# Finer phase steps merged by fractional position, and a reworked attention tail, in a four-layer attention/GLU kernel

## The chip, the cores and the metric

The kernel runs on one core of one Trainium2 chip. The time is the device time in microseconds of that core, one whole execution. The kernel before took 2078.02 us in the median of the twelve executions that ran beside the changed kernel (2074.32 to 2080.72).

Engines: TensorE (PE in the profile; PEld is its weight load), VectorE (DVE), ScalarE (ACT), GpSimd (POOL), SyncE (SP, which here only issues transfers).

## The reference, cut to what matters

```python
def _A_ref(x, wqkv, wo):              # attention, H = 32 heads of Dh = 32
    ...
    W, dil = 8, 2                     # each token sees 8 keys: itself, 2 back, 4 back, ... 14 back
    kg = k[:, :, idx_c, :]; vg = v[:, :, idx_c, :]
    logits = jnp.einsum("bhsd,bhswd->bhsw", q, kg) * scale     # masked where idx < 0
    attn = softmax(logits)
    o = jnp.einsum("bhsw,bhswd->bhsd", attn, vg)
    return o.reshape(B, S, D) @ wo

def _B_ref(x, W_gate, W_up, W_down):  # gated unit, F = 3584
    h = relu(x @ W_gate) * (x @ W_up)
    return h @ W_down

x = A_x                               # 1 x 2048 x 1024, bf16
x = x + _A_ref(layernorm(x), ...);  x = x + _B_ref(layernorm(x), ...)
x = x + _A_ref(layernorm(x), ...);  x = x + _B_ref(layernorm(x), ...)
```

## The kernel before

Each of the four layers works through four blocks of 512 tokens. An *item* is one layer and one block. Layers 0 and 2 are attention, 1 and 3 are the gated unit (GLU). An attention item has a phase (projections q, k, v; logits L; softmax) and a tail (expand, multiply by v, add, output projection). The tail is *deferred*: its steps are interleaved with the phase steps of the next item. So the tail of a layer's last attention item runs inside the first GLU block of the next layer; I call that block *mixed* and the other three *plain*.

The logits. `prod` is q times eight shifted copies of k, and TensorE sums it over the 32 dimensions of a head with a constant matrix `wide`, in column groups of 32:

```python
        def prod_red(c):                       # c: one of 8 groups of 4 heads
            ...
                prod = a_pool.tile([P, W, BLK], BF16, ...)
                nc.vector.tensor_tensor(prod[:], q..., k shifted 8 ways..., op=ALU.mult)   # cut
                for tq in range(TPB):          # 4
                    for w in range(W):         # 8
                        nc.tensor.matmul(Lt[32 * tq:32 * tq + 32, w, :], lhsT=wide[...],
                                         rhs=prod[:, w, tq * P:(tq + 1) * P], ...,
                                         tile_position=(0, 32 * tq))        # 32 matmuls of 128 columns
```

The tail. TensorE repeats the attention weights over a head's 32 dimensions (`E`, in PSUM, two buffers of two banks). VectorE multiplies E by shifted v, straight out of PSUM. GpSimd makes the first add of a tree of three, VectorE the other two:

```python
        def pv(c):
            ...
                for tqp in range(2):
                    tt = tl_pool.tile([P, 2, W, P], BF16, tag="t", ..., bufs=3)
                    for wh in range(2):
                        e = psum_e.tile([P, 2, BLK], F32, tag="E", name="E")      # 2 banks, bufs=2
                        for j in range(2):
                            nc.tensor.matmul(e[:, j, :], lhsT=eexp[...], rhs=a[...], ...)
                        nc.vector.tensor_tensor(tt[:, :, 4*wh:4*wh+4, :], e[:]..., vsh, op=ALU.mult)
                    nc.gpsimd.tensor_tensor(tt[:, :, 0:4, :], tt[:, :, 0:4, :], tt[:, :, 4:8, :], op=ALU.add)
                    nc.vector.tensor_tensor(tt[:, :, 0:2, :], tt[:, :, 0:2, :], tt[:, :, 2:4, :], op=ALU.add)
                    nc.vector.tensor_tensor(oT[...], tt[:, :, 0, :], tt[:, :, 1, :], op=ALU.add)
```

The order. Every engine executes its own instructions in the order of the compiled program. That follows the order in which the kernel emits them, but not strictly: some instructions are pulled forward where an engine would wait. Steps are coarse (one step is three projections, or a whole `pv`), and the layer norm of the next item goes in as one lump:

```python
            merged = _interleave(ph, prev_tl)          # by count
            pos = (len(merged) * 3) // 5
            merged = merged[:pos] + nln + merged[pos:] # layer norm of the next item, as a lump
            run(merged)
```

The down projection of the GLU (`down(half)`) accumulates in two tiles of two banks, from the same pool as E. Weights go through a ring of five slabs (`wring`), loaded by SyncE.

## Time and profile before

I cut the profiled execution into stages. A stage of attention runs from the first E matmul of one tail to the first E matmul of the next tail. A GLU block ends with the last residual add of its down projection. The first columns of each layer, before its first E, are the *heads*.

| before, us | heads (2) | attention items (6) | mixed GLU blocks (2) | plain GLU blocks (6) | sum |
|---|---|---|---|---|---|
| whole stage | 164.2 | 620.2 | 380.0 | 907.4 | 2071.8 |
| one of it | 99.3 and 64.9 | 103.4 | 190.0 | 151.2 | |

The page of the kernel before, its first and fourth part (busy time of the engines; the chain of work that ended last, by engine):

```profile
span 2075.1 us, 24471 instructions
...
PE 1891.8 (91%) x10496; PEld 862.3 (42%) x10496; DVE 824.0 (40%) x1050; ACT 528.6 (25%) x809; POOL 388.1 (19%) x311
...
PE 60%; DVE 16%; POOL 14%; issue 5%; ACT 4%; POOLq 0%; DVEq 0%; ACTq 0%
```

TensorE looks full over the whole span, yet it is only 60% of the chain. The average hides two regimes, which the table by stretches separates. Kernel before, one attention item and one plain GLU block; columns after the comma are the busy time of PE, PEld, DVE, ACT and POOL (with instruction counts), then the granted TensorE clock, the share of the DMA engines and GB/s:

```profile
197.10:303.30 106.20, 87.08 (x608) 39.82 (x608) 77.86 (x91) 32.16 (x50) 50.16 (x34) 0.95 0.24 80
750.60:903.30 152.70, 149.21 (x706) 67.95 (x704) 25.31 (x42) 33.76 (x53) 1.11 (x2) 0.99 0.46 145
```

The GLU block is TensorE, 149 of 153 us. In the attention item no engine is full: TensorE idles 19 us, VectorE 28. The kernel before, what engines waited for (total us, times, longest):

```profile
POOL t L309 <- DVE t L307: 532.0, 127, 52.0
...
DVE t L310 <- POOL t L309: 161.4, 120, 2.4
...
PE E L303 <- DVE t L307: 92.4, 78, 2.8
...
PE tp L186 <- ACT xn L182: 42.1, 16, 22.8
...
PE L L250 <- DVE prod L245: 13.6, 11, 2.0
```

Read upwards, this is a ring. E waits for VectorE's multiply (L307) to free its PSUM buffer. VectorE's queue is in order, so a multiply stands behind the small adds (L310) of the tile before it, and those wait for the GpSimd add (L309), which waits for the multiplies. VectorE's 161.4 us of waiting are about 20 us a tail; with 77.9 us of work that is 98 of the 106 us of an item.

The kernel before, groups by shape (busy us, mean ns of one, idle time before them and what ended it):

```profile
L309 POOL TENSOR_TENSOR t<-t 128x1024 bf16<-128x1024 bf16 x128 | 332.8, 2600 | 534.0 <-DVE t L307 532.0 <-DVE oT L311 2.0
L307 DVE TENSOR_TENSOR t<-E,v 128x1024 bf16<-128x1024 f32 x256 | 305.5, 1216 | 0.4 <-PE E L303 0.4
...
L245 DVE TENSOR_TENSOR prod<-q,k 128x4096 bf16<-128x4096 bf16 x64 | 155.8, 2434 | 68.8 <-ACT k L225 68.3
```

The kernel before, timeline of an item (start, duration, engine, line):

```profile
209.29 2.12 POOL L309 TENSOR_TENSOR t<-t 128x1024 bf16<-128x1024 bf16 x1 [1.53 <-DVE t L307]
209.32 4.23 DVE L245 TENSOR_TENSOR prod<-q,k 128x4096 bf16<-128x4096 bf16 x1
...
215.15 2.34 DVE L307 TENSOR_TENSOR t<-E,v 128x1024 bf16<-128x1024 f32 x2
216.51 2.12 POOL L309 TENSOR_TENSOR t<-t 128x1024 bf16<-128x1024 bf16 x1 [2.90 <-DVE t L307]
...
220.33 2.29 DVE L245 TENSOR_TENSOR prod<-q,k 128x4096 bf16<-128x4096 bf16 x1
220.37 4.23 POOL L309 TENSOR_TENSOR t<-t 128x1024 bf16<-128x1024 bf16 x1 [1.60 <-DVE t L307]
```

`prod` takes 2.29 us and the GpSimd add 2.12. Started together, whichever is second takes 4.23, about the sum of both: they do not share, one stands still. The multiplies out of PSUM at 215.15 are not slowed beside the GpSimd add (two in 2.34). The Trainium skill ("SBUF — State Buffer", section "SBUF: two separate sides") says just this: the port pair common to VectorE and GpSimd is an exclusive lock held for a whole instruction, taken by VectorE operations with two SBUF inputs against a GpSimd operation that reads SBUF. This trace agrees, with the numbers above.

The start of the kernel before (ACTq is ScalarE's instruction stream issuing transfers):

```profile
0.80 8.15 ACTq L121 DMA_DIRECT2D x<-in_A_x_dram  x8
...
9.04 1.28 ACT L160 ACT_TABLE_LOAD   x1 [9.04 <-DMA x<-in_A_x_dram]
```

### The profile page before, as it was taken

Reading aid. Unit: us, or ns where it says so; the run is one execution under the profiler, and the core shown is the slowest. Engines: PE = TensorE matmul, PEld = TensorE weight load, DVE = VectorE, ACT = ScalarE, POOL = GpSimd, SP = SyncE. Lnnn points to the kernel's source line nnn. Section 1 sums busy time; section 2 is a strip of 40 time slices with the busy share of each in tenths; the row PEclk is TensorE's granted clock in tenths of the full one; section 3 lists DMA queues with packets and bytes.
Section 4 is the critical chain, followed back from the end, with each engine's and each line's share of the span. In section 5 each row is a group of like instructions: output and inputs, shape, how many; then the busy total and the mean of one; then the engine's idle time right before and its main releaser. Section 6 shows DMA issues by size and latency. Waiting matters only on the chain.

```text
span 2075.1 us, 24471 instructions
## 1 busy us (share of the span) xinstructions
PE 1891.8 (91%) x10496; PEld 862.3 (42%) x10496; DVE 824.0 (40%) x1050; ACT 528.6 (25%) x809; POOL 388.1 (19%) x311
## 2 busy tenths in 40 slices
PE   4978787888999999999998788878999999999999
PEld 2534343433444444444444333333344444444444
DVE  1576767765121111111126777777541111210220
ACT  7623241412223023023033232323122130120110
POOL 1063535333000000000011535363320000000000
PEclk9999999999999999999999898999999999999999
DMA  5313131332444444444442131313335544544542
GB/s 186 123 61 102 61 102 61 102 112 92 152 152 129 155 149 142 152 152 135 143 142 68 55 102 61 102 62 121 114 113 161 162 133 152 172 140 153 174 142 92
DMA packets 246269, 253.44 MB, mean 122 GB/s; under 512 B 4400, under 2 KB 241968, under 8 KB 246160
## 3 DMA queue, kind: packets, MB, share of 16 engines
q1 hardware_dynamic: 245008, 249.77, 37.7%
q8 instruction: 82, 1.34, 0.3%
q10 hardware_dynamic: 1152, 2.10, 0.3%
q14 instruction: 27, 0.22, 0.0%
HBM read 247.46 MB, written 4.19 MB: 121 GB/s over the span
## 4 chain that ended last, share of the span: by engine, by line
PE 60%; DVE 16%; POOL 14%; issue 5%; ACT 4%; POOLq 0%; DVEq 0%; ACTq 0%
PE dacc L389 18%; PE acc_u L359 17%; PE acc_g L359 16%; POOL t L309 14%; DVE t L307 9%; PE acc_wo L323 2%; DVE t L310 2%; DVE prod L245 2%; PE acc_v L216 1%; PE acc_k L216 1%; PE acc_q L216 1%; ACT junk L160 1%; PE L L250 1%; ACT xn L182 1%; ACT xnT L187 1%
## 5 line engine op out<-in xcount | busy, mean ns | idle before, releaser
L359 PE MATMUL acc_u<-xnT,wu 128*128 128x512 bf16 x1792 | 428.8, 381 | 11.3 <-DVE hT L365 10.9
L359 PE MATMUL acc_g<-xnT,wg 128*128 128x512 bf16 x1792 | 435.6, 386 | 0.8 <-ACT xnT L187 0.6
L309 POOL TENSOR_TENSOR t<-t 128x1024 bf16<-128x1024 bf16 x128 | 332.8, 2600 | 534.0 <-DVE t L307 532.0
L389 PE MATMUL dacc<-wd,hT 128*128 128x512 bf16 x1792 | 388.1, 379 | 0.0
L365 DVE TENSOR_TENSOR hT<-acc_u,r 128x512 bf16<-128x512 f32 x224 | 154.8, 691 | 561.9 <-PE acc_u L359 511.0
L364 ACT ACTIVATE r<-acc_g 128x512 bf16<-128x512 f32 x224 | 133.5, 596 | 774.2 <-PE acc_g L359 774.2
L307 DVE TENSOR_TENSOR t<-E,v 128x1024 bf16<-128x1024 f32 x256 | 305.5, 1216 | 0.4 <-PE E L303 0.4
L359 PEld LDWEIGHTS <-wu 128*128 128x128 bf16 x1792 | 175.1, 98 | 227.4 <-issue 24.0
L359 PEld LDWEIGHTS <-wg 128*128 128x128 bf16 x1792 | 175.6, 99 | 220.6 <-issue 21.5
L389 PEld LDWEIGHTS <-hT 128*128 128x128 bf16 x1792 | 175.3, 98 | 211.5
L303 PE MATMUL E<-a,eexp 32*128 32x512 bf16 x512 | 104.8, 398 | 95.7 <-DVE t L307 92.4
L245 DVE TENSOR_TENSOR prod<-q,k 128x4096 bf16<-128x4096 bf16 x64 | 155.8, 2434 | 68.8 <-ACT k L225 68.3
L393 DVE TENSOR_TENSOR x<-dacc,x 128x512 bf16<-128x512 f32 x64 | 41.2, 686 | 349.8 <-PE dacc L389 349.8
L216 PE MATMUL acc_k<-xnT,wk 128*128 128x512 bf16 x512 | 141.3, 403 | 0.8 <-DVE x L326 0.8
L216 PE MATMUL acc_q<-xnT,wq 128*128 128x512 bf16 x512 | 131.6, 390 | 1.7 <-ACT xnT L187 1.7
L216 PE MATMUL acc_v<-xnT,wv 128*128 128x512 bf16 x512 | 130.6, 394 | 0.2 <-ACT q L220 0.2
L323 PE MATMUL acc_wo<-wo,oT 128*128 128x512 bf16 x512 | 114.6, 379 | 9.3 <-DVE x L326 9.3
L160 ACT ACTIVATE junk<-x 128x1024 bf16<-128x1024 bf16 x64 | 67.5, 1055 | 202.3 <-DVE x L393 194.0
L310 DVE TENSOR_TENSOR t<-t 128x512 bf16<-128x512 bf16 x128 | 54.4, 425 | 162.6 <-POOL t L309 161.4
L156 POOL MEMSET st<- 128x8 f32 x16 | 1.7, 111 | 607.6 <-DVE nvar L167 607.6
L303 PEld LDWEIGHTS <-eexp 32*128 32x128 bf16 x512 | 31.4, 92 | 186.3 <-issue 179.6
L250 PE MATMUL L<-prod,wide 128*32 128x128 bf16 x2048 | 89.0, 226 | 13.6 <-DVE prod L245 13.6
(49 smaller groups left out, 919.4 us busy)
## 6 DMA issues: line engine op xcount, KB each, us to landing
wg<-in_B_W_gate_dram SPq DMA_DIRECT2D x56, 1024.0 KB, 6.6
wu<-in_B_W_up_dram SPq DMA_DIRECT2D x56, 1024.0 KB, 5.3
wd<-in_B_W_down_dram SPq DMA_DIRECT2D x48, 1024.0 KB, 5.5
wq<-in_A_wqkv_dram SPq DMA_DIRECT2D x16, 1024.0 KB, 5.5
wk<-in_A_wqkv_dram SPq DMA_DIRECT2D x16, 1024.0 KB, 5.6
wv<-in_A_wqkv_dram SPq DMA_DIRECT2D x16, 1024.0 KB, 5.2
wo<-in_A_wo_dram SPq DMA_DIRECT2D x16, 1024.0 KB, 5.2
wd<-in_B_W_down_dram SPq DMA_DIRECT2D x16, 512.0 KB, 3.5
```

The source lines that it names most:

```text
L216: nc.tensor.matmul(acc[:], lhsT=wsl[:, kc, (c % 4) * P:(c % 4 + 1) * P], rhs=xnT[:, kc, :], start=(kc == 0), stop=(kc == KC - 1))
L245: nc.vector.tensor_tensor(prod[:], _ap(q, 0, [[0, W], [1, BLK]]), _ap(k, HALO, [[-DIL, W], [1, BLK]]), op=ALU.mult)
L250: nc.tensor.matmul(Lt[32 * tq:32 * tq + 32, w, :], lhsT=wide[:, 28 - 4 * c:60 - 4 * c], rhs=prod[:, w, tq * P:(tq + 1) * P], start=first, ...
L303: nc.tensor.matmul(e[:, j, :], lhsT=eexp[32 * tq:32 * tq + 32, c, :], rhs=a[32 * tq:32 * tq + 32, 4 * wh:4 * wh + 4, :], start=True, stop= ...
L307: nc.vector.tensor_tensor(tt[:, :, 4 * wh:4 * wh + 4, :], e[:].rearrange("p a (w t) -> p a w t", w=4), vsh, op=ALU.mult)
L309: nc.gpsimd.tensor_tensor(tt[:, :, 0:4, :], tt[:, :, 0:4, :], tt[:, :, 4:8, :], op=ALU.add)
L310: nc.vector.tensor_tensor(tt[:, :, 0:2, :], tt[:, :, 0:2, :], tt[:, :, 2:4, :], op=ALU.add)
L323: nc.tensor.matmul(acc[:], lhsT=st["oT"][c][:, t, :], rhs=wsl[:, c, :], start=(c == 0), stop=(c == KC - 1))
L359: nc.tensor.matmul(acc[:], lhsT=slabs[nm][:, kc, jl * P:(jl + 1) * P], rhs=xnT[:, kc, :], start=(kc == 0), stop=(kc == KC - 1))
L364: nc.scalar.activation(r[:], acc[:], ACT.Relu)
L365: nc.vector.tensor_tensor(hT[:, j, :], accs["u"][:], r[:], op=ALU.mult)
L389: nc.tensor.matmul(accs[t], lhsT=hT[:, j, t * P:(t + 1) * P], rhs=wsl[:, jl, :], start=(j == 0), stop=(j == FC - 1))
```

## The change

The intent is to take GpSimd out of the tail, to make TensorE's small matmuls cheaper, and to emit smaller steps in a better mixed order. It has these parts.

1. *Tail arithmetic.* E becomes one four-bank PSUM tile (one buffer). A new ScalarE copy `ecp` brings it to SBUF as bf16; VectorE multiplies from there and makes all three adds.
2. *Logits.* Eight matmuls of 512 columns in place of 32 of 128.
3. *Order.* Steps are one projection, half an expand, one tree, one output tile, one slab of the down projection. `merge` sorts them by fractional position; the layer norm is spread over 25% to 95% of an item.
4. *Room and the rest.* q, prod, softmax and hT tiles sit in a pool that lives for one layer, so that the new tiles fit; the weight ring has six slabs; the down accumulators are one four-bank tile; the 14-column halo copies of k and v go from GpSimd to VectorE; `prod` is emitted right after the projection of k, no longer together with its matmuls; at the start SyncE issues four loads of x and ScalarE twelve (eight each before).

```diff
-    wring = ctx.enter_context(tc.tile_pool(name="wring", bufs=5))
+    wring = ctx.enter_context(tc.tile_pool(name="wring", bufs=6))
-    psum_e = ctx.enter_context(tc.tile_pool(name="psum_e", bufs=2, space=bass.MemoryType.PSUM))
+    psum_e = ctx.enter_context(tc.tile_pool(name="psum_e", bufs=1, space=bass.MemoryType.PSUM))
@@ x loads
-        (nc.sync if t % 2 == 0 else nc.scalar).dma_start(xt[:], x_dram[t * P:(t + 1) * P, :])
+    for t in range(NT):
+        (nc.sync if t < TPB else nc.scalar).dma_start(x_tiles[t][:], x_dram[t * P:(t + 1) * P, :])
@@ logits
-                for tq in range(TPB):
-                    for w in range(W):
-                        nc.tensor.matmul(Lt[32 * tq:32 * tq + 32, w, :], ...
-                                         rhs=prod[:, w, tq * P:(tq + 1) * P],
+                for wh in range(2):
+                    for tq in range(TPB):
+                        nc.tensor.matmul(Lt[32 * tq:32 * tq + 32, 4 * wh:4 * wh + 4, :], ...
+                                         rhs=prod[:, 4 * wh:4 * wh + 4, tq * P:(tq + 1) * P],
@@ tail
-        def pv(c): ...                       # shown above
+        def expand(c, wh):
+                e = psum_e.tile([P, TPB, BLK], F32, tag="E", name="E")
+                for tq in range(TPB):
+                    nc.tensor.matmul(e[:, tq, :], lhsT=eexp[...], rhs=a[...], ...)
+                ecp = tl_pool.tile([P, TPB, 4, P], BF16, tag="ecp", name="ecp", bufs=3)
+                nc.scalar.copy(ecp[:], ev)
+                nc.vector.tensor_tensor(tt[:, :, 4 * wh:4 * wh + 4, :], ecp[:], vsh, op=ALU.mult)
+        def tree(c):
+                nc.vector.tensor_tensor(tt[:, :, 0:4, :], tt[:, :, 0:4, :], tt[:, :, 4:8, :], op=ALU.add)
+                nc.vector.tensor_tensor(tt[:, :, 0:2, :], tt[:, :, 0:2, :], tt[:, :, 2:4, :], op=ALU.add)
+                nc.vector.tensor_tensor(oT[:], tt[:, :, 0, :], tt[:, :, 1, :], op=ALU.add)
@@ down projection
-                e0 = psum_e.tile([P, 2, BLK], F32, tag="E", name="dacc0")
-                e1 = psum_e.tile([P, 2, BLK], F32, tag="E", name="dacc1")
+                    e0 = psum_e.tile([P, TPB, BLK], F32, tag="E", name="dacc")
@@ order
-            merged = _interleave(ph, prev_tl)
-            pos = (len(merged) * 3) // 5
-            merged = merged[:pos] + nln + merged[pos:]
-            run(merged)
+            run(merge([(0.0, 1.0, ph), (0.0, 1.0, prev_tl), (0.25, 0.95, nln)]))
... (the splitting of the steps, the pools and the halo copies are cut)
```

## The prediction

> **What bounds it now.** The page says TensorE 91% busy, VectorE 40%, GpSimd 19%, but the table by stretches shows two regimes. In the six plain GLU blocks (152 us each) TensorE is busy 149-150 of 152: 672 matmuls of 512 columns at 0.216 us (224 down matmuls took 48.36 us) are 145 us. In the attention items after the first (75-407 and about 1100-1430 us, three each layer, about 110 us an item) TensorE is busy only 82-83%, at a clock of 0.93-0.95. There the chain of waits is a ring: E matmuls, the PSUM multiply on VectorE (1.22 us), the GpSimd add (2.12 us, mean 2.60), VectorE adds, back to E (TensorE waited 92 us for that multiply). GpSimd is 14% of the chain. The timeline shows prod and the GpSimd add slowing one another: prod takes 2.29 us alone, 4.23 beside it. The GLU block that carries the last attention tail takes 191 us; the same ring is in it.
>
> **What changes, costed.**
> - GpSimd's first add moves to VectorE; GpSimd busy 388 -> below 40 us.
> - E goes through a new ScalarE copy (128x2048 fp32 to bf16). A 1024-wide activation took 1.06 us, so about 1.95 us by extrapolation, x128 = 250 us: ScalarE 529 -> about 770 us.
> - The multiply then reads two bf16 SBUF operands. The Trainium skill ("VectorE: DVE Perf Modes", the perf-mode tier table) gives tensor_tensor 2x for bf16 in SBUF, 1x with PSUM; this trace agrees: 0.56 ns per element for prod, 1.19 for the PSUM multiply. So about 1.15 us per 2048, and tree adds of 1.15, 0.6 and 0.35: VectorE per item about 69 us, 700 us in all.
> - L: 32 matmuls of 128 columns (1.27 us) become 8 of 512, four column groups at once, about 0.55 us: 6 us an item, 46 in all.
> - Finer steps: layer-norm stages are spread over 25-95% of a block, so the 6 us stretch of transposes waiting for xn in each GLU block (652-659 us) mostly goes.
> - A single four-bank E buffer, so each E waits for the copy of the one before; in the down halves the order puts seven matmuls of the next block into that gap, so it should cost little.
> - At the start ScalarE issues twelve loads, not eight (8 took 8.2 us), and its first activation moves 4 us later.
>
> **Sum for one attention item.** TensorE: 256 matmuls 55.3, E 16 x 0.54, L 4.4, transposes 2.4: 71 us. VectorE 69, ScalarE 65. Three engines nearly level, so not 71: E-to-copy-to-E turns (0.6 + 2.0, plus a 0.58 k/q/v copy ahead in the queue) and the softmax latency (8 us, partly filled) add about 12: 83 us against 110.
>
> **Where it lands.** Six attention items -27 each: -165. Two mixed GLU blocks 191 -> about 173: -36. Six plain GLU blocks -3 each: -18. Two first items: -10. Start +4. Total about -225: **1850 us, 80% range 1805 to 1905**; faster by over 2% 0.97, within 0.02, slower 0.01.
>
> **What would show it.** Right: GpSimd gone from the chain; TensorE over 90% busy in attention items; multiplies near 1.15 us; prod at 2.2-2.3 throughout; item period 77-88 us; plain GLU blocks 148-150; mixed about 173. The largest TensorE wait in attention should be E on the ScalarE copy.
>
> **What would make it wrong.** If the E copy costs well over 2 us, or ScalarE's in-order queue (layer-norm statistics, 1.25 us each) delays it, TensorE stalls twice per c and items stay near 95 us: about 1910. If VectorE's queue lags so that prod comes late, likewise. If the four-group L matmuls do not overlap (0.216 each, 1.7 us per c), add 75 us: above 1905. If the level engines overlap better, items near 75 us give about 1800.

## The result, and the profile after

The changed kernel takes 1898.74 us in the median of eight executions (1898.01 to 1900.99). The ratio is 0.9141, 95% interval 0.9132 to 0.9150. A ratio here is the mean time of one kernel's fast runs over that of the other's in the same rounds, so it is not quite the ratio of the medians. The output is correct, as it is for every kernel below.

By stages (profiled executions, one of each kind in parentheses; the four stages add up to the sum):

| us | heads | attention items | mixed | plain | sum |
|---|---|---|---|---|---|
| before | 164.2 | 620.2 (103.4) | 380.0 (190.0) | 907.4 (151.2) | 2071.8 |
| after | 157.6 | 488.8 (81.5) | 349.5 (174.8) | 897.2 (149.5) | 1893.0 |
| difference | -6.6 | -131.4 | -30.5 | -10.2 | -178.8 |

The page of the kernel after, the same two parts:

```profile
span 1896.5 us, 21085 instructions
...
PE 1770.1 (93%) x8960; PEld 772.5 (41%) x8960; DVE 737.3 (39%) x986; ACT 751.3 (40%) x937; POOL 20.6 (1%) x39
...
PE 72%; DVE 14%; ACT 9%; DMA 3%; issue 1%; POOL 0%; DVEq 0%; ACTq 0%; POOLq 0%
```

GpSimd has left the chain, and ScalarE carries 223 us more than before. The kernel after by stretches: the same attention item, the same plain block, and the two halves of that item:

```profile
183.50:264.90 81.40, 72.67 (x416) 28.59 (x416) 66.58 (x83) 59.86 (x65) 1.01 (x1) 0.98 0.32 104
672.60:822.60 150.00, 147.57 (x706) 67.54 (x705) 25.01 (x43) 33.86 (x53) 1.01 (x1) 1.00 0.47 147
183.50:224.20 40.70, 35.17 (x208) 12.12 (x208) 39.35 (x50) 31.45 (x27) 1.01 (x1) 0.96 0.25 78
224.20:264.90 40.70, 37.50 (x210) 16.47 (x209) 27.23 (x34) 28.41 (x39) 0.00 (x0) 1.00 0.39 130
```

TensorE is now at 89% in the item. The halves show where the rest is: in the first, VectorE works 39.35 of 40.70 us, in the second 27.23. The kernel after, waits:

```profile
PE tp L190 <- ACT xn L186: 32.6, 2, 29.6
PE L L255 <- DVE prod L242: 31.3, 23, 2.7
...
PE acc_g L378 <- DMA wg<-in_B_W_gate_dram: 11.4, 6, 2.1
...
PE E L309 <- ACT ecp L315: 6.7, 15, 0.8
```

The ring is gone: E waited 92.4 us for VectorE's multiply and now waits 6.7 for the ScalarE copy. The layer norm's transposes now wait twice, 29.6 us of it once at the start of the kernel, where before there were 16 waits (22.8 us of them at the start). One wait has grown: L waits 31.3 us for `prod`, which is VectorE's queue, where it waited 13.6. One wait is new: the gate matmul waits six times for its weights. The kernel after, groups:

```profile
L315 ACT CAST ecp<-E 128x2048 bf16<-128x2048 f32 x128 | 239.3, 1870 | 85.9 <-PE E L309 84.9
...
L316 DVE TENSOR_TENSOR t<-ecp,v 128x2048 bf16<-128x2048 bf16 x128 | 155.9, 1221 | 40.6 <-ACT ecp L315 40.5
...
L242 DVE TENSOR_TENSOR prod<-q,k 128x4096 bf16<-128x4096 bf16 x64 | 146.4, 2287 | 68.2 <-ACT k L229 68.2
...
L322 DVE TENSOR_TENSOR t<-t 128x2048 bf16<-128x2048 bf16 x64 | 78.1, 1221 | 0.8
```

The multiply of 2048 elements takes 1.22 us, where two of 1024 out of PSUM took 2.43. `prod` is at 2.29 throughout. The Trainium skill ("VectorE: DVE Perf Modes", section "The perf-mode tier table (the rule you actually need)") gives 1224 ns for `tensor_tensor` on 2048 bf16 elements in SBUF, and no speed-up with PSUM: the trace agrees to 3 ns. For the copy, the cycle table of the same page (section "The TRN2 errata — SBUF-src ops pay a fixed extra latency per instruction") has 172 cycles plus one per element at 1.2 GHz for ScalarE from PSUM; my estimate from it for 2048 is 1.85 us, measured 1.87.

The kernel after, timeline around the middle of a down projection (SPq is SyncE issuing):

```profile
483.83 6.64 PE L409 MATMUL dacc<-wd,hT 128*128 128x512 bf16 x30
...
487.05 0.37 SPq L143 DMA_DIRECT2D wg<-in_B_W_gate_dram  x1
...
492.58 2.94 PE L378 MATMUL acc_g<-xnT,wg 128*128 128x512 bf16 x7 [2.11 <-DMA wg<-in_B_W_gate_dram]
```

The compiled order puts seven gate matmuls of the next block between the two halves of the down projection, because the second half waits for the accumulator tile. Their weights could only be requested once a slab of the ring was free, 5.5 us earlier, and were 2.1 us late. The start of the kernel after:

```profile
0.79 15.00 ACTq L123 DMA_DIRECT2D x<-in_A_x_dram  x12
...
15.82 1.28 ACT L162 ACT_TABLE_LOAD   x1 [15.82 <-DMA x<-in_A_x_dram]
```

The granted clock moves too, and this bears on every comparison below. In these traces it is either 1.0 or 0.5, and it is at 0.5 in stretches of about 3.4 us or more (27 us at the longest, in e6). Before, one such stretch in a plain block, and the stretch before it; after, the down projection above, and the seven late gate matmuls with the first of the second half (columns as before, the clock is the third number from the end):

```profile
648.50:656.50 8.00, 5.49 (x37) 2.83 (x35) 1.38 (x2) 3.68 (x5) 0.00 (x0) 1.00 0.50 160
657.00:660.00 3.00, 2.90 (x19) 1.69 (x17) 0.00 (x0) 2.88 (x4) 0.00 (x0) 0.50 0.66 220
```

```profile
484.00:490.40 6.40, 6.40 (x30) 2.74 (x28) 0.00 (x0) 0.00 (x0) 0.00 (x0) 1.00 0.32 98
493.00:496.00 3.00, 3.00 (x8) 1.03 (x7) 0.00 (x0) 0.00 (x0) 0.00 (x0) 0.50 0.70 241
```

Seven gate matmuls took 2.94 us there, 0.42 us each, where one takes 0.216 us at full clock. In the kernels before and after, every such stretch had a TensorE gap of at least 1.0 us in the 9 us ahead of it. So a stall seems to cost more than its own length; that the gap causes the lower clock is not shown by an experiment. Worked out from the clock records of the traces, TensorE was at work at half clock for 104 us before and 38 us after. Half of that is lost, so at most about 33 of the 179 us gained are clock. This is an upper estimate, since TensorE would have waited for other engines in part of it.

### The profile page after: what moved, and what is told of

Same layout as the page of the kernel before. It is cut to its first block, busy times and chain, and to the rows that moved or that the text cites. A ratio compares the mean times of both kernels' runs of the same rounds, so it can differ in the third digit from the quotient of the medians.

```text
span 1896.5 us, 21085 instructions
## 1 busy us (share of the span) xinstructions
PE 1770.1 (93%) x8960; PEld 772.5 (41%) x8960; DVE 737.3 (39%) x986; ACT 751.3 (40%) x937; POOL 20.6 (1%) x39
## 3 DMA queue, kind: packets, MB, share of 16 engines
q8 instruction: 70, 1.15, 0.2%
## 4 chain that ended last, share of the span: by engine, by line
PE 72%; DVE 14%; ACT 9%; DMA 3%; issue 1%; POOL 0%; DVEq 0%; ACTq 0%; POOLq 0%
PE acc_g L378 20%; PE acc_u L378 20%; PE dacc L409 19%; PE acc_wo L340 5%; DVE t L316 4%; DVE prod L242 4%; ACT ecp L315 2%; PE acc_v L220 2%; DVE t L322 2%; PE acc_k L220 2%; PE acc_q L220 2%; DMA wg<-in_B_W_gate_dram 2%; ACT junk L162 1%; ACT junk L164 1%; DVE t L323 1%
## 5 line engine op out<-in xcount | busy, mean ns | idle before, releaser
L378 PE MATMUL acc_g<-xnT,wg 128*128 128x512 bf16 x1792 | 427.1, 381 | 14.5 <-DMA wg<-in_B_W_gate_dram 11.4
L315 ACT CAST ecp<-E 128x2048 bf16<-128x2048 f32 x128 | 239.3, 1870 | 85.9 <-PE E L309 84.9
L242 DVE TENSOR_TENSOR prod<-q,k 128x4096 bf16<-128x4096 bf16 x64 | 146.4, 2287 | 68.2 <-ACT k L229 68.2
L316 DVE TENSOR_TENSOR t<-ecp,v 128x2048 bf16<-128x2048 bf16 x128 | 155.9, 1221 | 40.6 <-ACT ecp L315 40.5
L340 PE MATMUL acc_wo<-wo,oT 128*128 128x512 bf16 x512 | 123.8, 383 | 16.2 <-DVE oT L325 4.9
L191 ACT COPY xnT<-tp 128x1024 bf16<-128x1024 bf16 x64 | 65.1, 1019 | 43.7 <-PE tp L190 43.5
L340 PEld LDWEIGHTS <-oT 128*128 128x128 bf16 x512 | 48.6, 98 | 81.2 <-issue 22.3
L186 ACT ACTIVATE xn<-x,nb,rstd 128x1024 bf16<-128x1024 bf16 x64 | 80.0, 1253 | 0.9 <-DVE k L231 0.9
L322 DVE TENSOR_TENSOR t<-t 128x2048 bf16<-128x2048 bf16 x64 | 78.1, 1221 | 0.8
L343 DVE TENSOR_TENSOR x<-acc_wo,x 128x512 bf16<-128x512 f32 x64 | 43.9, 689 | 84.8 <-PE acc_wo L340 84.8
```

Source lines behind the costliest of these rows:

```text
L186: nc.scalar.activation(xn[:], xt[:], ACT.Identity, scale=holder["rstd"][:, t:t + 1], bias=holder["nb"][:, t:t + 1])
L242: nc.vector.tensor_tensor(prod[:], _ap(q, 0, [[0, W], [1, BLK]]), _ap(tl, HALO, [[-DIL, W], [1, BLK]]), op=ALU.mult)
L315: nc.scalar.copy(ecp[:], ev)
L316: nc.vector.tensor_tensor(tt[:, :, 4 * wh:4 * wh + 4, :], ecp[:], vsh, op=ALU.mult)
L322: nc.vector.tensor_tensor(tt[:, :, 0:4, :], tt[:, :, 0:4, :], tt[:, :, 4:8, :], op=ALU.add)
L340: nc.tensor.matmul(acc[:], lhsT=st["oT"][c][:, t, :], rhs=wsl[:, c, :], start=(c == 0), stop=(c == KC - 1))
```

## The experiments

Two theories. **A**: the gain is the broken ring; VectorE's cheap multiply and GpSimd's absence let the tail run beside the projections, and the order matters second. **B**: the gain is the order; fine steps and a spread layer norm keep TensorE fed, and the tail arithmetic would have been hidden anyway. Later experiments ask what still bounds the changed kernel. Where the time of TensorE's work at half clock (38 us in the changed kernel) differs much, I give it; half of the difference is the most that the clock can have contributed. All twelve were timed in three rounds, four runs each; stages are of each run's profiled execution.

| run | edit, from the changed kernel | median us | ratio to before [95%] | heads | items | mixed | plain |
|---|---|---|---|---|---|---|---|
| after | | 1898.74 | 0.9141 [0.9132, 0.9150] | 157.6 | 488.8 | 349.5 | 897.2 |
| e1_coarse | coarse steps, layer norm as a lump | 1919.65 | 0.9243 [0.9229, 0.9257] | 161.1 | 477.5 | 357.1 | 918.5 |
| e2_sched_only | old tail and old accumulators | 2083.26 | 1.0029 [1.0014, 1.0044] | 160.8 | 652.5 | 378.3 | 885.0 |
| e3_L128 | logits in 128 columns | 1916.67 | 0.9229 [0.9213, 0.9244] | 167.8 | 492.2 | 353.5 | 896.1 |
| e4_ln_lump | only the layer norm as a lump | 1951.03 | 0.9394 [0.9380, 0.9408] | 165.6 | 504.8 | 354.3 | 919.3 |
| e5_pooladd | first add on GpSimd | 2050.37 | 0.9869 [0.9854, 0.9884] | 158.1 | 628.3 | 358.2 | 898.9 |
| e6_psummul | no ScalarE copy | 2007.87 | 0.9664 [0.9650, 0.9679] | 159.2 | 594.3 | 354.6 | 896.4 |
| e7_spread | tail's expands end at 0.88 | 1861.80 | 0.8961 [0.8946, 0.8976] | 157.2 | 454.7 | 347.1 | 896.1 |
| e8_E2bank | two accumulators of two banks | 1874.77 | 0.9024 [0.9011, 0.9037] | 162.8 | 476.9 | 345.1 | 885.0 |
| e9_spread_E2 | e7 and e8 | 1846.15 | 0.8889 [0.8874, 0.8904] | 161.7 | 455.5 | 338.4 | 884.8 |
| e10_best | e9, x loads from GpSimd | 1835.16 | 0.8834 [0.8821, 0.8847] | 151.3 | 457.3 | 338.4 | 885.1 |
| e11_ring7 | seven slabs | 1888.79 | 0.9090 [0.9076, 0.9104] | 157.1 | 487.2 | 347.8 | 891.6 |
| e12_coarse_att | e10 with coarse attention steps | 1864.86 | 0.8981 [0.8966, 0.8996] | 150.4 | 466.1 | 358.1 | 885.2 |

The most direct test, the new tail put alone into the kernel before, could not be made: it did not fit in SBUF without the pool that lives for one layer. So e1 and e2 start from the changed kernel and undo one side each. Neither undoes all of its side: both keep the halo copies on VectorE and the earlier `prod`.

### e1_coarse: the new arithmetic in the old order

```diff
-            steps.append(proj(c, "q")) ... (c, "k"), (c, "v")
+            steps.append(p3)      # q, k, v in one step; likewise pv, wo4, down4, do_ln
-            run(merge([(0.0, 1.0, ph), (0.0, 1.0, prev_tl), (0.25, 0.95, nln)]))
+            merged = _interleave(ph, prev_tl)
+            pos = (len(merged) * 3) // 5
+            run(merged[:pos] + nln + merged[pos:])
```

> The changed kernel with its new arithmetic (ScalarE copy of E, multiply from SBUF, whole add tree on VectorE, 512-wide L) but with the old coarse steps and the old interleave. Theory A (the old ring over GpSimd and the PSUM multiply was the loss, so the arithmetic carries the gain): about 1925 us, within 15 to 45 us of the changed kernel. Rival B (the finer, fractionally merged schedule carries it): 2000 us or more. Under A the GLU blocks lose about 3 us each to the layer-norm lump.

Measured: 1919.65, that is 21 us slower than the changed kernel and 157 faster than before (7.57% of 2078). This is inside the expectation of theory A. The attention items are, if anything, shorter than the changed kernel's (477.5 against 488.8); what is lost is in the GLU blocks. TensorE works 72 us at half clock, so up to 17 of the 21 us can be clock.

### e2_sched_only: the new order with the old tail

```diff
-        def expand(c, wh):  ... def tree(c): ...
+        def expand(c, tqp): ... # the old loop: E of 2x2 banks, multiply from PSUM, first add on GpSimd
```

> The changed kernel with its fine schedule, wide L and six-slab ring, but the old attention tail: multiply straight from PSUM, first add on GpSimd, E in two buffers of two banks. Theory A: the ring stays, attention items stay near 100 us, about 2030 to 2055 us. Rival B: below 1980 us.

Measured: 2083.26, no gain (ratio 1.0029), and 28 us above the range that theory A gave. The ring is back. The waits of this run, then one group of it:

```profile
PE E L312 <- DVE t L316: 87.4, 86, 2.5
...
PE L L255 <- DVE prod L242: 46.1, 22, 3.3
```

```profile
L233 DVE COPY v<-v 128x14 bf16<-128x14 bf16 x48 | 38.9, 810 | 0.0
```

TensorE waited 87.4 us for E on VectorE's multiply, against 92.4 before, and 46.1 for `prod`. The order by itself helped the plain blocks (885.0 against 907.4) and lost it again in the attention items: they took 652.5 us, before 620.2; the mixed blocks are nearly unchanged (378.3 against 380.0). One piece of that loss shows above: the v halo copy of 14 columns, now on VectorE, takes 810 ns in the mean here (166 in the median, 2107 at the longest, where a GpSimd add is beside it) and 167 in the changed kernel. All halo copies together cost VectorE 31 us more than there. TensorE's work at half clock in the items is 80 us, 67 before.

The run also weighs the lock. `prod` is at 2.29 us here and the GpSimd add at 2.15, so the two hardly meet, and yet the items are no shorter. This speaks against the slowing of one by the other as the main cost of the ring, and for the waiting in the queues.

Theory B falls, as a whole: the order with the old tail gains nothing, while everything but the order (e1) gains about 157 of 179 us. What the order would gain with the halo copies left on GpSimd was not run. Note that e2 still has the 512-column logits, the sixth slab and the new loads; so even those gain nothing while the ring stands.

### e3_L128: the logits back to 32 matmuls of 128 columns

```diff
-                        nc.tensor.matmul(Lt[32 * tq:32 * tq + 32, 4 * wh:4 * wh + 4, :],
+                        nc.tensor.matmul(Lt[32 * tq:32 * tq + 32, w, :],     # w in range(8)
```

> The changed kernel with the L matmuls back to 32 of 128 columns (about 0.7 us more TensorE time per head group, 46 us over the kernel). Theory A2 (in the first half of each attention item VectorE paces TensorE, which has slack there): only 10 to 25 us slower than the changed kernel. Rival (TensorE is the critical engine throughout): 40 to 50 us slower.

Measured: +18 us. One group of 32 matmuls takes 1.27 us from its start to the next instruction and one of eight 0.54 to 0.55, so TensorE's own saving is about 0.72 us x 64 = 46 us. Only 18 reach the total. The heads, where no tail runs beside, pay nearly in full (10 of 11.5 us); the six items pay 3 of 35. There TensorE was often waiting for VectorE anyway (TensorE's wait for `prod` falls from 31.3 to 21.9 us). The clock takes another part: TensorE works only 17 us at half clock in this run, 38 in the changed kernel, which can give back up to 11 us.

### e4_ln_lump: the layer norm as a lump at 0.6

```diff
-            run(merge([(0.0, 1.0, ph), (0.0, 1.0, prev_tl), (0.25, 0.95, nln)]))
+            run(merge([(0.0, 1.0, ph), (0.0, 1.0, prev_tl), (0.6, 0.6, nln)]))
```

> The changed kernel with the layer-norm steps all at fraction 0.6, instead of spread over 0.25 to 0.95. If spreading removes the gap of transposes waiting for xn (6 us, of which about 3 are real loss, per block): 20 to 45 us slower than the changed kernel. If the scheduler hides the lump anyway: within 5 us.

Measured: +52 us: plain +22, items +16, heads +8, mixed +5. TensorE works 84 us at half clock, so up to 22 of the 52 us can be clock. In the plain blocks the loss is 3.7 us each. In the items it is not settled: e1 has the lump too, with coarse steps, and its items are the shorter ones. Where the lump falls between the steps seems to matter as much as that it is one; no run separates this.

With the accumulators (e8) the plain blocks form a square of two times two, which closes almost exactly (the kernel before differs from the other cells in its five slabs and coarse steps too):

| plain blocks, six together, us | layer norm as a lump | spread |
|---|---|---|
| two accumulators of two banks | 907.4 (before) | 885.0 (e2, e8) |
| one of four banks | 918.5 (e1), 919.3 (e4) | 897.2 (after) |

So spreading the layer norm gives 22 us here, and the one accumulator tile takes 11 to 12 back. The changed kernel shows only the remainder, 10. Of the 22 us, up to 8 to 10 can be clock: in the plain blocks TensorE works 19 us at half clock before, 20 in e4, 3 in the changed kernel and none in e2 and e8.

### e5_pooladd: the first add back on GpSimd, all else new

```diff
-                nc.vector.tensor_tensor(tt[:, :, 0:4, :], ..., tt[:, :, 4:8, :], op=ALU.add)
+                nc.gpsimd.tensor_tensor(tt[:, :, 0:4, :], ..., tt[:, :, 4:8, :], op=ALU.add)
```

> The changed kernel with only the first tree add put back on GpSimd. GpSimd's add of 2048 elements would take about 5 us beside VectorE's two-input work (2.6 us per 1024 in the kernel before), 64 of them, and VectorE's prod beside it nearly doubles. E no longer waits for the add, so the ring is open: about 1930 to 1950 us if only the contention matters; above 2000 us if GpSimd itself was what the ring turned on.

Measured: 2050.37, a cost of 152 us. This is the second of the two expectations (above 2000 us): contention alone does not explain it, and `prod` kept its 2.29 us. The groups of this run, then one wait:

```profile
L322 POOL TENSOR_TENSOR t<-t 128x2048 bf16<-128x2048 bf16 x64 | 305.2, 4768 | 359.0 <-DVE t L316 172.6 <-DVE k L233 118.4 <-DVE v L233 68.0
...
L323 DVE TENSOR_TENSOR t<-t 128x1024 bf16<-128x1024 bf16 x64 | 44.3, 692 | 236.8 <-POOL t L322 236.8
```

```profile
PE L L255 <- DVE prod L242: 87.2, 26, 7.2
```

I had counted 1.22 us of VectorE work saved for each add. But the next add stands right behind it in VectorE's queue and waits 3.7 us each time (236.8 us over 64), because the GpSimd add takes 4.77 us. TensorE's wait of L on `prod` grows from 31.3 to 87.2 us, since `prod` sits in the same queue. The GpSimd add itself took 4.0 to 4.1 us in 34 of its 64 cases, and 5.0 or 6.0 in the 30 where a multiply or `prod` of VectorE ran beside it; those kept their times. TensorE works 115 us at half clock, so up to 38 of the 152 us can be clock. The cheap multiply from SBUF is worth little while this wait stays. The parts of the change need one another.

### e6_psummul: the multiply straight from PSUM again, no ScalarE copy

```diff
-                ecp = tl_pool.tile([P, TPB, 4, P], BF16, tag="ecp", name="ecp", bufs=3)
-                nc.scalar.copy(ecp[:], ev)
-                nc.vector.tensor_tensor(tt[:, :, 4 * wh:4 * wh + 4, :], ecp[:], vsh, op=ALU.mult)
+                nc.vector.tensor_tensor(tt[:, :, 4 * wh:4 * wh + 4, :], ev, vsh, op=ALU.mult)
```

> The changed kernel with only the ScalarE copy taken out: VectorE multiplies straight from the four-bank E in PSUM. Each multiply goes from 1.22 to about 2.3 us on VectorE and holds the only E buffer meanwhile: VectorE per item 67 + 17 = 84 us. If VectorE paces the items: about 97 us an item, 2010 to 2040 us. If the copy was only a detour: within 20 us of the changed kernel.

Measured: 2007.87, +109 us, just below the expected 2010 to 2040. The multiply of this run, then a wait:

```profile
L314 DVE TENSOR_TENSOR t<-E,v 128x2048 bf16<-128x2048 f32 x128 | 292.2, 2283 | 2.8 <-PE E L309 2.8
```

```profile
PE E L309 <- DVE t L314: 84.3, 70, 2.8
```

It takes 2283 ns instead of 1221, 136 us of VectorE work over 128, and E waits 84.3 us for it. TensorE works 69 us at half clock, so up to 15 of the 109 us can be clock. Taking GpSimd out without taking PSUM out of the multiply is worth about 70 us (2078 to 2008, together with the rest of the change); the two together 179. This run shows also what the ScalarE copy buys: it costs 1.87 us on an engine that had room, and saves 1.06 on the one that had none.

### e7_spread: the tail's expands end at 0.88 of the item

The first half of an item was VectorE at 97%, the second at 67%. The phase's last step, the softmax, comes at the end, and so does the tail's output projection, in which VectorE has only residual adds to make. If the output projection is pressed into the last 12%, the expands and trees can be spaced wider.

```diff
-            run(merge([(0.0, 1.0, ph), (0.0, 1.0, prev_tl), (0.25, 0.95, nln)]))
+            na = 3 * KC if prev_tl else 0
+            run(merge([(0.0, 1.0, ph), (0.0, 0.88, prev_tl[:na]), (0.88, 1.0, prev_tl[na:]), (0.25, 0.95, nln)]))
```

> The changed kernel with the expand and tree steps of the attention tail spread over fractions 0 to 0.88 and the output projection over 0.88 to 1, instead of both evenly by step count (where expand and tree end at 0.75). In the changed kernel VectorE is busy 39.4 of the first 40.7 us of an item and 27.2 of the second. Theory: that uneven load is what keeps items at 81.4 us against 71 us of TensorE work; then items fall to 75 to 79 us and the whole to 1860 to 1885 us. Rival (softmax and buffer turns set the item): within 8 us of 1899.

Measured: 1861.80, -37 us, inside the expectation. The two halves of an item of this run:

```profile
249.60:289.10 39.50, 36.15 (x210) 13.58 (x210) 33.72 (x43) 32.51 (x36) 1.01 (x1) 1.00 0.31 105
289.10:328.70 39.60, 37.14 (x220) 16.50 (x218) 32.64 (x39) 28.79 (x35) 0.00 (x0) 1.00 0.39 122
```

VectorE works 33.7 and 32.6 us, where it was 39.4 and 27.2, and the items fall from 81.5 to 75.8 us in the mean. TensorE's wait for `prod` falls from 31.3 to 11.2 us. So it was where VectorE's load falls in the item, and not its sum, that held the changed kernel's items. Not all of the 37 us are the wait itself: TensorE works 7 us at half clock here and 38 in the changed kernel, so up to 16 us can be the clock that came back when the stalls went.

### e8_E2bank: two accumulators of two banks

```diff
-                e = psum_e.tile([P, TPB, BLK], F32, tag="E", name="E")          # bufs=1
+                eh = [psum_e.tile([P, 2, BLK], F32, tag="E", name=f"E{h}") for h in range(2)]   # bufs=2
-                nc.scalar.copy(ecp[:], ev)
+                for h in range(2):
+                    nc.scalar.copy(ecp[:, 2 * h:2 * h + 2, :, :], eh[h]...)
-                    e0 = psum_e.tile([P, TPB, BLK], F32, tag="E", name="dacc")
+                    e0, e1 = ...  # dacc0, dacc1 of two banks, as in the kernel before
```

> The changed kernel with the PSUM accumulators in two buffers of two banks (two ScalarE copies of 1024 per E, and the down accumulators as before) instead of one of four. Theory: the one four-bank buffer makes the order put seven matmuls of the next block between the down halves, and their weights arrive 2 us late; without that, plain GLU blocks fall from 150.0 to 148.0 us, as the schedule-only run had. Attention items: 81 us if E turns do not matter, or shorter by up to 2 us. Whole: 1878 to 1890 us.

Measured: 1874.77, -24 us, slightly better than expected: plain -12, items -12, mixed -4, heads +5. The wait of the gate matmul for its weights is gone from the list. The trace shows the two down halves running on with no gate matmul between them; as I read it, the second half can start in the first freed tile, so nothing has to be pulled forward. In the items VectorE is as uneven as before (39.3 of the first 40.4 us), yet they are 12 us shorter. TensorE works 7 us at half clock in this run, none of it in the items, so much of these 12 us can be clock. Splitting the copy in two costs ScalarE 5 us in all (756.2 against 751.3).

### e9_spread_E2: e7 and e8 together

> The spread tail (expand and tree over 0 to 0.88) and the two-bank accumulators together. The two act in different blocks (spread: attention items -34 us; two-bank: plain GLU blocks -12 us, items and mixed blocks about -16 us of which part overlaps with the spread). If they add fully: 1838 us; if the item part overlaps: 1843 to 1852 us. Above 1860 would mean that they undo one another.

Measured: 1846.15, inside the expectation. The edits are those of e7 and e8. They are worth 53 us together, 37 and 24 alone: nearly additive. They overlap in the items (-33 together, -34 and -12 alone).

### e10_best: the loads of x from GpSimd's queue as well

```diff
-        (nc.sync if t < TPB else nc.scalar).dma_start(x_tiles[t][:], ...)
+        (nc.sync if t < TPB else nc.gpsimd).dma_start(x_tiles[t][:], ...)
```

> As the run before, and the later twelve x tiles are loaded from the GpSimd queue, not the ScalarE queue. In the changed kernel ScalarE issues twelve loads in 15 us before its first activation at 15.8 us; in the kernel before, 8 loads, first activation at 9.0. Theory: the head shortens by 6 to 10 us, the rest stays. Rival (weights and x tiles share the DMA engines, so the head is set by landings, not by issue): within 3 us of the run before.

Measured: 1835.16, -11 us, of which the heads are 10.4. The start of this run:

```profile
0.79 1.28 ACT L162 ACT_TABLE_LOAD   x1 [0.79 <-PEq L505]
...
3.42 1.06 ACT L162 ACTIVATE junk<-x 128x1024 bf16<-128x1024 bf16 x1 [1.35 <-DMA x<-in_A_x_dram]
```

ScalarE's table load begins at 0.79 us instead of 15.82, as nothing stands in its queue. This is the fastest kernel: 0.8834 of before, and 3.3% below the changed kernel (1835.16 for 1898.74).

### e11_ring7: a seventh slab

```diff
-    wring = ctx.enter_context(tc.tile_pool(name="wring", bufs=6))
+    wring = ctx.enter_context(tc.tile_pool(name="wring", bufs=7))
... (one buffer fewer of oT, ecp and r, for room)
```

> The changed kernel with seven weight slabs in the ring (and ecp, r and oT one buffer fewer, to make room). Theory: the 2 us wait for a gate slab in each GLU block comes from its slot being freed only by the third down slab; with seven slots the wait of 11 us in all goes, plain blocks fall from 150.0 to about 148.2 us, whole about 1885 to 1889 us. Rival (the wait is DMA bandwidth): no change.

Measured: 1888.79, -10 us, inside the expectation, and the gate matmul's wait is gone from the list. The plain blocks take 891.6, nearly half way to e8's 885.0. The late slab is therefore the cause of the 11.4 us, and the pulled-forward matmuls are what made it matter. The other half of e8's gain in the plain blocks, 6.6 us, has no cause shown.

### e12_coarse_att: the best version with coarse attention steps

e1's short items suggested coarse steps in attention.

```diff
+            steps.append(p3); ... steps.append(pv); ... steps.append(wo4)     # as in e1; down and layer norm stay fine
```

> The combined version (two-bank accumulators, x tiles from the GpSimd queue, layer norm spread) with the attention steps coarse again, as in the kernel before: q, k and v of a head group in one step, expand and tree in one, half an output projection in one, merged evenly by step count, so that expand and tree end at 0.8 by themselves; no explicit 0.88. Theory: the grain of the attention steps is worth nothing, only where VectorE's work falls counts: 1835 to 1855 us. Rival (fine steps are needed in the items): 1870 us or more.

Measured: 1864.86, a miss, between the theory's range and the rival's: 30 us slower than e10, of which 20 are in the mixed blocks and 9 in the items. Fine steps do matter once the ring is gone, most of all where a tail is mixed with a long GLU phase. The fraction at which the expands end differs a little between the two, so the 9 us in the items are not cleanly the grain's.

## Why the prediction was right or wrong, point by point

The total lies inside the range, near its upper edge: 1899 for 1850. The direction and the mechanism were right; the gain was 179 us where 225 were forecast.

| term | forecast | measured | by |
|---|---|---|---|
| six attention items | -165 (110 to 83 each) | -131 (103.4 to 81.5) | stages |
| two mixed blocks | -36 (191 to 173) | -30.5 (190.0 to 174.8) | stages |
| six plain blocks | -18 | -10.2 | stages |
| heads and start | -10 + 4 | -6.6 | stages |
| sum | -225 | -179 | |

- **The term that was mis-sized is the item of before.** The forecast of the item after (83) was good to 1.5 us, in part by luck: the groups of E were counted 3 us an item too long, half clock (about 2 us an item) was not in the sum, and the 12 us of waiting were right in size but were laid to the E copy, which TensorE hardly waited for. But "about 110 us an item" before was a window of 332 us divided by three, and the window's edges took in part of a neighbouring stage. From first E to first E the items were 97.9, 106.2, 106.1, 97.8, 106.2 and 106.1, mean 103.4. Six times the difference is 34 to 40 us, most of the 46 by which the sum was off.
- **The step "so it should cost little" was wrong.** It said that the seven matmuls put into the gap of the down halves would hide the single accumulator. They were there, but their weights were up to 2.1 us late in six cases, 11.4 us in all; e8 and e11 confirm the cause. The layer norm's own gain in the plain blocks was as forecast or better: the square above gives 3.7 us each, against the forecast 3.
- **The ring** was read rightly: GpSimd is gone from the chain, `prod` is at 2.29 us throughout, E no longer waits on VectorE's multiply. e2, e5 and e6 show that each part of the ring, left in place, takes back most of the gain.
- **The largest wait was named wrongly.** I expected E on the ScalarE copy; it waited 6.7 us. It was L on `prod`, 31.3 us, VectorE's queue, which stood only among the risks. With VectorE's load spread (e7) it falls to 11.2 us. It also falls to 15.6 us in e8, where the load is as uneven as before, so the uneven load is not shown to be its only cause.
- **Costs of single operations**: multiply 1.22 us (1.15 forecast), copy 1.87 (1.95), group of L matmuls 0.54 to 0.55 (0.55), group of four E matmuls 0.33 from its start to the next instruction (0.54, taken from L; some 3 us an item too much), VectorE 737 us in all (about 700), ScalarE 751 (about 770), GpSimd 20.6 (below 40). TensorE is busy 89% of an item (over 90 forecast).
- **The 46 us of L** were part of the item's sum as TensorE time. e3 shows that 18 of them reached the total (up to 11 more may be hidden by the clock, as said there). The prediction's sum took this into account only in that it kept 12 us for waiting.
- **The start** moved the right way and further: the first activation came at 17.1 us, not 10.3, so 7 us later where 4 were forecast. e10 shows that this was avoidable.
- **The clock** was named for the items of before (0.93 to 0.95), but the sum for the item after took every matmul at full clock (0.216 us). The clock of the items rose from 0.94 to 0.97 only.

Left open: why the items of e1, with coarse steps and a lump, are shorter than the changed kernel's, while the lump alone (e4) lengthens them. The record has one hint: TensorE waits for `prod` only 12.7 us in e1, 31.3 in the changed kernel. What the clock is worth apart from the stalls that come before it is open too; no run holds one and changes the other.

## What to carry to other kernels

Where no engine is full, look for a ring through in-order queues, and break it as a whole: taking GpSimd out without the cheap multiply, or the reverse, or only reordering the steps, gained a fraction or nothing. Tabulate the granted clock by stage too, before a gain is put down to one cause. Afterwards tabulate each engine's load over parts of a repeating item: an engine at 97% in one half and 67% in the other is a matter of order, and spacing its steps was worth 37 us for two lines of code. When a change merges two accumulators into one, check what the instruction order pulls into the gap, and whether its data can be there in time.

## What the Trainium skill lacked or had wrong

- "DMA: Bandwidth & Descriptors", section "Issuing engines are not separate DMA queues", says that issuing from several engines only saves sequencer time, "usually small relative to the DMA itself". Here the issuing time was what cost: twelve loads kept ScalarE's queue for 15.00 us before its first computing instruction, and moving them to an idle engine made the kernel 11 us faster (e10 against e9). The page lacks the warning that the issuing engine's own compute stands behind its issues.
- "TensorEngine Tiling (Array Packing)", section "PSUM Bottleneck", warns that tiling speeds TensorE and not the emptying of PSUM. The runs agree: four E matmuls ran together in 0.40 us (timeline of the changed kernel), and one ScalarE copy of their output took 1.87. The page gives no measured time for column-tiled matmuls with narrow moving data: the same logits took 1.27 us as 32 column-tiled matmuls of 128 columns, and 0.54 to 0.55 as eight of 512.
- "SBUF — State Buffer" describes the lock correctly, but has no figure for how it delays copies as small as these: VectorE's copies of 14 columns of v took 810 ns in the mean and up to 2107 ns beside GpSimd adds (e2), and 167 ns without them (changed kernel).
- No page treats the grain of the emitted order between in-order engines: coarse attention steps cost 30 us in the best version (e12), and the new order gained nothing while the ring stood (e2).
